# Float64 weights to float32: the high word scaled on ScalarE in place of squared, and one VectorE operation less a piece

## The chip, the cores and the metric

The kernel runs on one core of a Trainium2 chip. A core has TensorE (PE, with its weight loads PEld), VectorE (DVE), ScalarE (ACT), GpSimd (POOL) and SyncE (SP, which here issues all the DMAs), each with an in-order queue of its own; they meet through semaphores. The metric is the time of one execution on the device in microseconds (us). Lower is better.

## The reference

Three stages follow one another. A causal attention (4 batches, 8 heads, 576 positions, head size 64) with a cumulative bias; a mixing block and a feed-forward network (FFN); and a second block of four gated attention experts.

```
x  = attention(q, k, v, s)                       # 4 x 576 x 512
u  = x + ((x^T @ U) @ V)^T                       # mix, rank 32
x  = u + relu(u @ w_ch1) @ w_ch2                 # FFN, 512 -> 2048 -> 512
y  = sum over 2 of 4 experts of gate * (causal attention of x with wq, wk, wv) @ wo
```

`U`, `V`, `w_ch1` and `w_ch2` arrive as float64 (the scale factor of the drawn inputs makes them so) and are used as float32 values. The kernel gets their bits as 64-bit integers.

## The kernel before

**Float64 to float32.** A double has 11 bits of exponent, a float 8. The kernel reads each number as two 32-bit words. The words of a piece of 128 x 256 numbers (the tile `c_raw`, 256 KB) are brought by one DMA. `f32_stages` gives the piece's steps: `s0` (line 103) issues the load; `p0` (line 106, ACT) squares the high word read as a float, into `c_mk`; `p1` (line 109, DVE) keeps the high word where that square is at least a threshold and puts zero elsewhere, into `c_h`; then `v0` to `v4` (lines 113, 118, 122, 127, 131, all DVE) shift the bits up by three, put the two top bits back, isolate sign and exponent into `c_z`, scale the low word by it, and add the two parts. `v5` (ACT, line 198) rounds the sum to the matmul's format (`wh`), and `v6` (POOL, line 201) takes the rest (`wl`): every product is made of three matmuls, wh by x, wl by x and wh by the rest of x.

**The order of the steps.** The pieces form a stream (`f32_stream`). For each piece there are eight steps, by one of two tables: `STREAM` while the first attention runs, `PLAIN` in the FFN. A pair (d, x) in a table is step x of the piece d places ahead: x from 0 is v0 to v6, and -3, -2, -1 are s0, p0, p1. So a load is issued two pieces ahead, and p0 and p1 run one piece ahead.

**Attention stage.** `Attn.run` has 170 iterations (32 heads of 5 row tiles, and 10 more for the lag): scores on PE, masked row minimum on DVE (line 373), exponential on ACT (line 380), normalisation on POOL (line 391), and ten iterations later transposes on PE (lines 403, 406), their eviction, and every tenth iteration the product with V (line 432). Behind each iteration `fillers` puts other work: steps of the stream (one an iteration, two in iterations 41 to 69), preparation of the next head pair, and through `background` tasks of the mix and of the FFN for three of the 16 slices of hidden units (f = 0, 1, 2). An FFN task is a first product of one slice and one chunk of 288 tokens (`hps`, 12 matmuls, line 294) or a second product of one output block (`facc`, 9 matmuls, line 308). A task is only taken when its slice's weights have been wholly converted in program order (`full[f]`); what is left over when iteration 161 comes is put there in one go, ahead of the last transposes.

**FFN stage.** Slices 3 to 15 go in groups of 2, 3, 3, 3 and 2. A slot is one first product (line 826, 12 matmuls) and one second product of an earlier slot (line 844, 12 matmuls); the chunk's four accumulators are evicted by DVE (line 851) after its last slot of the group, and the next chunk's second products wait for that. While one group runs, the next one's weights are converted, and the stream's steps are spread over the slots in proportion (`conv`). The first group of two has 22 slots, 6 of which are left over from slices 0 to 2, and it converts three slices.

A `manual_schedule` keeps the order that the code writes on each engine.

Of the kernel before, what the change touches and what calls it, by code (L numbers as in the profile page):

```python
# [34 lines left out]
HALF = S // 2  # L35
# [10 lines left out]
FA = 3  # L46
GROUPS = [2, 3, 3, 3, 2]

PLAIN = (((0, 0),), ((0, 1),), ((0, 2), (1, -2)), ((0, 3),), ((0, 4), (2, -3)), ((1, -1),), ((0, 5),), ((0, 6),))
STREAM = (((0, 0),), ((-1, 5),), ((0, 1),), ((0, 2), (1, -2)), ((-1, 6),), ((0, 3),), ((0, 4), (2, -3)), ((1, -1),))  # L50
FAST = (40, 70)

ENGA = ('vaaaaa', 'aavaav')
# [14 lines left out]
HIENG = "av"  # L68
BG = (1, 1, 0, 2, 1)
ULF = "vggg"  # L70
TINY = 1.5 * 2.0 ** -15


def cp(nc, eng, out, in_):
# [11 lines left out]
def f32_stages(nc, pool, width, load, m, n, name, use=None, dest=None, fixed={}):  # L86

    t_ = {}  # L90

    def tile_(tag, dt, bufs=1):
        if tag in fixed:
            t_[tag] = fixed[tag][:m, :n].bitcast(dt)
            return t_[tag]
        t_[tag] = pool.tile([P, width], dt, tag=tag, name=f"{tag}_{name}", bufs=bufs)[:m, :n]
        return t_[tag]

    def s0():
        raw = pool.tile([P, width], I64, tag="c_raw", name=f"c_raw_{name}", bufs=2)[:m, :n]  # L100
        load(raw)
        words = raw.bitcast(U32).rearrange("p (n w) -> p n w", w=2)
        t_["low"], t_["high"] = words[:, :, 0], words[:, :, 1].bitcast(F32)

    def p0():
        nc.scalar.activation(out=tile_("c_mk", F32), in_=t_["high"], func=AF.Square)

    def p1():
        nc.vector.scalar_tensor_tensor(out=tile_("c_h", F32), in0=t_["c_mk"], scalar=TINY * TINY,
                                       in1=t_["high"], op0=OP.is_ge, op1=OP.mult)  # L110

    def v0():
        nc.vector.tensor_scalar(out=tile_("c_a", U32, 2), in0=t_["c_h"].bitcast(U32), scalar1=3, scalar2=0x3FFFFFF8,
                                op0=OP.logical_shift_left, op1=OP.bitwise_and)

    def v1():

        nc.vector.scalar_tensor_tensor(out=t_["c_a"], in0=t_["c_h"].bitcast(U32), scalar=0xC0000000, in1=t_["c_a"],
                                       op0=OP.bitwise_and, op1=OP.bitwise_or)

    def v2():
        nc.vector.tensor_scalar(out=tile_("c_z", U32), in0=t_["c_a"], scalar1=0xFF800000, scalar2=None,
                                op0=OP.bitwise_and)

    def v3():

        nc.vector.scalar_tensor_tensor(out=t_["c_h"], in0=t_["low"], scalar=2.0 ** -52, in1=t_["c_z"].bitcast(F32),
                                       op0=OP.mult, op1=OP.mult)

    def v4():  # L130
        nc.vector.tensor_tensor(out=t_["c_a"].bitcast(F32) if use else dest(), in0=t_["c_h"],
                                in1=t_["c_a"].bitcast(F32), op=OP.add)

    def v5():
        if use:
            t_["u"] = use(t_["c_a"].bitcast(F32))
            next(t_["u"])

    def v6():
        if use:  # L140
            next(t_["u"], None)

    return [s0, p0, p1, (v0, v1, v2, v3, v4, v5, v6)]


def f32_stream(jobs, order):

    n = len(jobs)
    for i in range(-2, n + 1):
        for pieces in order:  # L150
            l = [jobs[i + d][3][x] if x >= 0 else jobs[i + d][x + 3] for d, x in pieces if 0 <= i + d < n]
            if l:
                def step(l=l):
                    for f in l:
# [5 lines left out]
def fused_kernel(ctx, tc, qk, v, s, u, vv, w12, wp, out):  # L160
# [349 lines left out]
    with ExitStack() as cx:  # L510
# [699 lines left out]
```

## Time and profile before

| | us |
|---|---|
| time, median of 3 runs | 871.74 |
| lowest and highest run | 869.67, 872.11 |
| profiled execution, first to last instruction (its span) | 870.1 |
| PE, DVE, ACT, POOL busy in it | 814.2, 603.4, 466.9, 310.6 |

The page states no time of its own for the profiled execution beside its span. The span is within the three runs and 1.6 us under their median; the rest of an execution lies around it. A busy PE is not a PE at its peak, since the matmuls overlap in the records: in a stretch without any wait it runs 153 matmuls in 20 us, and the count beside the busy time says more than the share.

### The profile page before, as it was taken

To read this page: it belongs to the slowest core of one execution; us is meant where nothing else is said; L and a number is where in the kernel's file an instruction comes from. 1 tells how busy PE (TensorE), PEld (TensorE's weight loads), DVE (VectorE), ACT (ScalarE), POOL (GpSimd) and SP (SyncE) were. 2 spreads that over 40 slices of the span, in tenths; PEclk is the share of its full clock that TensorE was granted. 3 is DMA by queue.
4 is the path that set the end of the run, shared out by engine and by line. 5 is a ranking of instruction groups with operands and counts; after the bars stand their busy time and mean duration, and the time that the engine had idled before them with its cause. 6 is when DMAs were issued, how large, how long until landed. Compare 5 with 4: busy or idle time off the path is not lost.

```text
span 870.1 us, 17626 instructions
## 1 busy us (share of the span) xinstructions
PE 814.2 (94%) x6068; PEld 747.8 (86%) x6068; DVE 603.4 (69%) x1759; ACT 466.9 (54%) x1384; POOL 310.6 (36%) x468
## 2 busy tenths in 40 slices
PE   3887898999999999999999999999999999999997
PEld 2665676898987889999999999999999988999875
DVE  8687788877687349985885887577446785656541
ACT  6587668866677344323442443333323567666672
POOL 5444255444334324323432342233233123232241
PEclk9898899999999999999999999999999999999999
DMA  7888479687570151111111121112000122112221
GB/s 206 224 212 213 127 187 241 165 210 194 157 195 16 56 188 37 49 50 25 53 48 48 49 61 50 49 43 57 1 1 1 30 42 43 37 55 50 67 64 61
DMA packets 36945, 79.66 MB, mean 92 GB/s; under 512 B 4792, under 2 KB 7992, under 8 KB 36856
## 3 DMA queue, kind: packets, MB, share of 16 engines
q1 hardware_dynamic: 36856, 78.53, 33.7%
q8 instruction: 48, 0.79, 0.4%
q14 instruction: 41, 0.34, 0.1%
HBM read 38.80 MB, written 8.40 MB: 54 GB/s over the span
## 4 chain that ended last, share of the span: by engine, by line
PE 72%; DVE 13%; ACT 5%; DMA 4%; issue 3%; POOL 1%; SPq 1%; DVEq 0%; POOLq 0%; ACTq 0%
PE hps L826 18%; PE facc L844 17%; PE pv L432 9%; PE qkp L1054 5%; PE t L403 4%; PE ops L1077 3%; PE facc L308 3%; PE vps L987 3%; PE qk L362 3%; PE qk L363 2%; PE hps L294 2%; DVE P L373 2%; PE t L406 2%; DMA c_raw_w<-in_w_dram 2%; DMA L<-Cd 2%
## 5 line engine op out<-in xcount | busy, mean ns | idle before, releaser
L278 POOL TENSOR_TENSOR ul<-uT,uh 128x288 fp32r<-128x288 f32 x126 | 103.8, 843 | 175.5 <-ACT uh L277 158.9
L380 ACT ACTIVATE P<-P,stat 64x64 f32<-64x64 f32 (+4 forms) x240 | 133.8, 558 | 43.4 <-DVE stat L373 39.8
L391 POOL TENSOR_SCALAR P<-P,stat 64x64 f32<-64x64 f32 (+4 forms) x160 | 100.9, 646 | 132.0 <-DVE stat L386 88.0
L373 DVE CUSTOM_DVE_ANT_0 P<-qk,mask 64x64 f32<-64x64 f32 (+4 forms) x240 | 116.4, 486 | 45.6 <-PE qk L363 28.8
L362 PE MATMUL qk<-R,L 128*128 128x288 f32 (+4 forms) x288 | 96.7, 340 | 23.1 <-DVE L L573 9.8
L830 ACT ACTIVATE hh<-hps 128x288 fp32r<-128x288 f32 x110 | 44.9, 408 | 135.2 <-PE hps L826 135.0
L76 ACT ACTIVATE pt<-t 64x64 f32<-64x64 f32 (+5 forms) x304 | 89.9, 336 | 42.0 <-PE t L406 36.6
L844 PE MATMUL facc<-hh,wh 128*128 128x288 f32 x376 | 111.2, 296 | 0.6 <-DVE aT L851 0.6
L826 PE MATMUL hps<-uh,wl 128*128 128x288 f32 x376 | 111.2, 296 | 0.0
L826 PE MATMUL hps<-ul,wh 128*128 128x288 f32 x376 | 111.1, 296 | 0.0
L826 PE MATMUL hps<-uh,wh 128*128 128x288 f32 x376 | 111.0, 295 | 0.0
L831 DVE SCALAR_TENSOR_TENSOR hl<-hps,hh 128x288 fp32r<-128x288 f32 x110 | 50.1, 455 | 87.7 <-ACT hh L830 87.4
L844 PE MATMUL facc<-hh,wl 128*128 128x288 f32 x376 | 110.9, 295 | 0.0
L844 PE MATMUL facc<-hl,wh 128*128 128x288 f32 x376 | 110.8, 295 | 0.0
L403 PE MATMUL t<-ident,P 128*128 128x128 f32 x480 | 89.6, 286 | 15.6 <-ACT pt L76 5.6
L363 PE MATMUL qk<-R,L 68*128 68x288 f32 (+9 forms) x288 | 89.1, 315 | 1.2 <-DMA L<-Cd 1.2
L391 POOL TENSOR_SCALAR P<-P,stat,pt 64x64 f32<-64x64 f32 (+4 forms) x80 | 48.5, 620 | 113.3 <-DVE stat L386 57.6
L362 PEld LDWEIGHTS qk<-R,L 128*128 128x128 f32 x288 | 57.3, 199 | 31.3 <-issue 14.9
L403 PEld LDWEIGHTS t<-ident,P 128*128 128x128 f32 x480 | 58.7, 143 | 28.9 <-issue 15.6
L432 PE MATMUL pv<-pt,V 128*64 128x288 f32 (+4 forms) x752 | 80.6, 364 | 0.0
L201 POOL TENSOR_TENSOR wl<-c_a_w,wh 128x256 fp32r<-128x256 f32 x56 | 43.6, 778 | 93.4 <-ACT wh L198 90.9
L432 PEld LDWEIGHTS pv<-pt,V 128*64 128x64 f32 x752 | 52.2, 147 | 27.8 <-issue 7.7
(194 smaller groups left out, 2196.7 us busy)
## 6 DMA issues: line engine op xcount, KB each, us to landing
c_raw_w<-in_w_dram SPq DMA_DIRECT2D x64, 256.0 KB
uT<-in_qk_dram SPq DMA_DIRECT2D x15, 576.0 KB
L<-HI SPq DMA_DIRECT2D x28, 288.0 KB
R<-HI SPq DMA_DIRECT2D x28, 288.0 KB
V<-in_v_dram SPq DMA_DIRECT2D x16, 320.0 KB
R<-uT SPq DMA_DIRECT2D x14, 288.0 KB
L<-uT SPq DMA_DIRECT2D x14, 288.0 KB
aD<-stage SPq DMA_DIRECT2D x6, 576.0 KB
```

The lines of the kernel that those rows point to most:

```text
L76: nc.scalar.activation(out=out, in_=in_, func=AF.Copy)
L278: eng.tensor_tensor(out=l_, in0=src, in1=h_.bitcast(F32), op=OP.subtract)
L362: nc.tensor.matmul(ps[:, bk, :w], lhsT=q1[:, rows], rhs=k1[:, c0:c0 + w], start=True, stop=False)
L363: nc.tensor.matmul(ps[:, bk, :w], lhsT=q2[:, rows], rhs=k2[:, c0:c0 + w], start=False, stop=True)
L373: nc.vector.tensor_tensor_reduce(out=po, in0=view, in1=mk, scale=-1.0, scalar=3.0e38, op0=OP.add, op1=OP.min, accum_out=stat[P - M:, 0, t: ...
L380: nc.scalar.activation(out=po, in_=po, func=AF.Exp, scale=-1.0, bias=stat[P - M:, 0, t:t + 1], accum_out=stat[P - M:, 1, t:t + 1])
L391: nc.gpsimd.tensor_scalar(out=pv, in0=pv, scalar1=stat[r0:, 2, t:t + 1], scalar2=1.0 if gate is None else gate(t)[r0:], op0=OP.mult, op1=O ...
L403: nc.tensor.transpose(ps[:, P * kb:P * kb + P], Pn[:, c0:c0 + P], ident)
L432: nc.tensor.matmul(ps[64 * hh:64 * hh + 64, half, lo - a:e - a], lhsT=V(hh, kb), rhs=pt[:, PST * kb + lo:PST * kb + e], start=kb == 0, sto ...
L826: nc.tensor.matmul(ps, lhsT=w[:, 0, cs], rhs=x, start=i == 0, stop=i == 11)
L831: nc.vector.scalar_tensor_tensor(out=hl, in0=ps, scalar=0.0, in1=hh.bitcast(F32), op0=OP.max, op1=OP.subtract)
L844: nc.tensor.matmul(accs[c][d], lhsT=w[:, 1, cs], rhs=x, start=f == fs[0] and i == 0, stop=f == fs[-1] and i == 2)
```

## The change

`p0` now multiplies the high word, read as a float, by 2^-112 (ACT, `Copy` with a scale), into `c_g`. That takes 112 from the float's exponent field, so that after the shift by three the exponent is a float32's. `p1` is gone, and with it `c_mk`. `v0` only shifts, without the mask that was its second operation, and `v1` puts back one top bit and not two; both read `c_g`. `c_h` is now written by `v3` alone. The tables have seven steps a piece.

```diff
-PLAIN = (((0, 0),), ((0, 1),), ((0, 2), (1, -2)), ((0, 3),), ((0, 4), (2, -3)), ((1, -1),), ((0, 5),), ((0, 6),))
+PLAIN = (((0, 0),), ((0, 1),), ((0, 2), (1, -1)), ((0, 3),), ((0, 4), (2, -2)), ((0, 5),), ((0, 6),))
...
     def p0():
-        nc.scalar.activation(out=tile_("c_mk", F32), in_=t_["high"], func=AF.Square)
-
-    def p1():
-        nc.vector.scalar_tensor_tensor(out=tile_("c_h", F32), in0=t_["c_mk"], scalar=TINY * TINY,
-                                       in1=t_["high"], op0=OP.is_ge, op1=OP.mult)
+
+        nc.scalar.activation(out=tile_("c_g", F32), in_=t_["high"], func=AF.Copy, scale=2.0 ** -112)
 
     def v0():
-        nc.vector.tensor_scalar(out=tile_("c_a", U32, 2), in0=t_["c_h"].bitcast(U32), scalar1=3, scalar2=0x3FFFFFF8,
-                                op0=OP.logical_shift_left, op1=OP.bitwise_and)
+        nc.vector.tensor_scalar(out=tile_("c_a", U32, 2), in0=t_["c_g"].bitcast(U32), scalar1=3, scalar2=None,
+                                op0=OP.logical_shift_left)
...
-    return [s0, p0, p1, (v0, v1, v2, v3, v4, v5, v6)]
+    return [s0, p0, (v0, v1, v2, v3, v4, v5, v6)]
```

`STREAM` loses its `p1` in the same way. Lines behind the change are four lower than before (831 is 827, 851 is 847, 294 is 290).

What moves on DVE, in the FFN's first group, around the eviction of chunk 4 (`facc_4`). The names `c_a`, `c_h`, `c_z`, `c_mk`, `c_raw` are those of the steps above, with the piece's column behind them. Before:

```order
L127 SCALAR_TENSOR_TENSOR c_h_w_0_4579<-c_raw_w_0_4472,c_z_w_0_4635 128x256
L131 TENSOR_TENSOR c_a_w_0_4583<-c_h_w_0_4579,c_a_w_0_4583 128x256
L109 SCALAR_TENSOR_TENSOR c_h_w_256_4643<-c_mk_w_256_4637,c_raw_w_256_4577 128x256
L831 SCALAR_TENSOR_TENSOR hl_4_4659<-hps_4_4645,hh_4_4658 128x288
L851 TENSOR_TENSOR aT<-facc_4_0_4602,aT 128x288
L851 TENSOR_TENSOR aT<-facc_4_1_4603,aT 128x288
L851 TENSOR_TENSOR aT<-facc_4_2_4604,aT 128x288
L851 TENSOR_TENSOR aT<-facc_4_3_4605,aT 128x288
L113 TENSOR_SCALAR c_a_w_256_4682<-c_h_w_256_4643 128x256
L118 SCALAR_TENSOR_TENSOR c_a_w_256_4682<-c_h_w_256_4643,c_a_w_256_4682 128x256
L122 TENSOR_SCALAR c_z_w_256_4685<-c_a_w_256_4682 128x256
L831 SCALAR_TENSOR_TENSOR hl_0_4703<-hps_0_4689,hh_0_4702 128x288
```

The same place now:

```order
L123 SCALAR_TENSOR_TENSOR c_h_w_0_4610<-c_raw_w_0_4446,c_z_w_0_4606 128x256
L127 TENSOR_TENSOR c_a_w_0_4554<-c_h_w_0_4610,c_a_w_0_4554 128x256
L827 SCALAR_TENSOR_TENSOR hl_4_4632<-hps_4_4618,hh_4_4631 128x288
L847 TENSOR_TENSOR aT<-facc_4_0_4574,aT 128x288
L847 TENSOR_TENSOR aT<-facc_4_1_4575,aT 128x288
L847 TENSOR_TENSOR aT<-facc_4_2_4576,aT 128x288
L847 TENSOR_TENSOR aT<-facc_4_3_4577,aT 128x288
L109 TENSOR_SCALAR c_a_w_256_4652<-c_g_w_256_4608 128x256
L114 SCALAR_TENSOR_TENSOR c_a_w_256_4652<-c_g_w_256_4608,c_a_w_256_4652 128x256
L118 TENSOR_SCALAR c_z_w_256_4655<-c_a_w_256_4652 128x256
L123 SCALAR_TENSOR_TENSOR c_h_w_256_4659<-c_raw_w_256_4550,c_z_w_256_4655 128x256
L827 SCALAR_TENSOR_TENSOR hl_0_4675<-hps_0_4661,hh_0_4674 128x288
```

The step between the sum of one piece and the eviction (line 109 of before, with `c_mk`) is gone; nothing else changes places there.

What moves on PE, in iteration 83 of the first attention. `qk` are scores, `t` transposes. Before, iteration 83 ends and iteration 84 begins with no FFN task between them:

```order
L362 MATMUL qk_3_1748<-R_0_121,L_0_119 128x448
L363 MATMUL qk_3_1748<-R_0_124,L_0_122 128x448
L403 MATMUL t_3_1751<-ident,P_114 128x128 x4
L362 MATMUL qk_4_1760<-R_0_121,L_0_119 128x288
L363 MATMUL qk_4_1760<-R_0_124,L_0_122 128x288
```

Now the first product of slice 2 stands there, and behind it the second products:

```order
L358 MATMUL qk_3_1756<-R_0_121,L_0_119 128x448
L359 MATMUL qk_3_1756<-R_0_124,L_0_122 128x448
L399 MATMUL t_3_1759<-ident,P_114 128x128 x4
L290 MATMUL hps_2_1768<-uh_0_1404,wh_1347 128x288
L290 MATMUL hps_2_1768<-ul_0_1405,wh_1347 128x288
L290 MATMUL hps_2_1768<-uh_0_1404,wl_1348 128x288
```

Slice 2's first product moves from iteration 99 to 83. The FFN tasks of the second batch end in iteration 126 and not 129; iterations 127 to 132 have no task of mix or FFN now, and 133 to 150 those of the third batch's mix alone. The third batch's FFN starts in iteration 151 and not 156. Ahead of the last transposes 2 first and 4 second products are left over, where there were 3 and 8. The stream's last conversion step stands near iteration 136, where it stood near iteration 159.

## Rows read from the trace of the kernel before

**Rows 1.** Stages: stretch and length, busy PE, PEld, DVE, ACT, POOL (count), clock, DMA, GB/s.
```profile
10.00:142.00 132.00, 108.86 (x720) 84.88 (x721) 106.97 (x360) 96.81 (x309) 59.14 (x90) 0.91 0.76 198
142.00:165.00 23.00, 20.21 (x156) 16.50 (x153) 18.91 (x64) 19.16 (x64) 12.87 (x21) 1.00 0.93 234
165.00:221.00 56.00, 54.39 (x444) 49.73 (x444) 44.13 (x143) 39.56 (x126) 23.49 (x36) 1.00 0.71 192
221.00:265.00 44.00, 43.29 (x348) 38.46 (x348) 34.45 (x115) 30.56 (x97) 16.54 (x27) 1.00 0.56 150
265.00:300.00 35.00, 33.56 (x260) 29.54 (x257) 19.50 (x57) 16.98 (x52) 13.21 (x21) 1.00 0.09 27
324.00:384.00 60.00, 57.28 (x423) 56.10 (x422) 54.15 (x123) 21.91 (x60) 20.65 (x25) 1.00 0.16 41
384.00:660.00 276.00, 276.00 (x2080) 276.00 (x2079) 191.13 (x453) 101.83 (x275) 91.79 (x116) 1.00 0.15 40
```

**Rows 2.** Who waited for whom on PE, 330 to 400: total us, times, longest.
```profile
PE facc L844 <- DVE aT L851: 1.8, 2, 1.2
PE hps L826 <- DVE hl L831: 0.9, 2, 0.7
```

**Rows 3.** DVE's timeline near 357: start, us, operation, tiles, shape.
```profile
356.77 0.43 DVE L109 SCALAR_TENSOR_TENSOR c_h_w<-c_mk_w,c_raw_w 128x256 f32<-128x256 f32 x1
...
357.48 1.17 DVE L851 TENSOR_TENSOR aT<-facc,aT 128x288 f32<-128x288 f32 x3
```

**Rows 4.** PE's timeline, its two longest waits of that stage [idle before <- releaser].
```profile
345.34 0.40 PE L826 MATMUL hps<-uh,L 128*128 128x288 f32 x1 [0.68 <-DVE hl L831]
...
357.98 0.40 PE L844 MATMUL facc<-hh,L 128*128 128x288 f32 x1 [1.17 <-DVE aT L851]
```

**Rows 5.** The step that goes, by line: busy us, mean ns | idle before.
```profile
L109 DVE SCALAR_TENSOR_TENSOR c_h_w<-c_mk_w,c_raw_w 128x256 f32<-128x256 f32 x44 | 22.6, 514 | 2.3 <-ACT c_mk_w L106 0.5
L109 DVE SCALAR_TENSOR_TENSOR pt<-pt,c_raw_w 128x256 f32<-128x256 f32 x20 | 8.2, 411 | 0.1
```

**Rows 6.** The same line by itself: ns of one, least/median/longest.
```profile
L109 DVE SCALAR_TENSOR_TENSOR c_h_w<-c_mk_w,c_raw_w x44: 407/426/1066, 325.9 to 609.7; 128x256 f32<-128x256 f32 x44
```

**Rows 7.** That line's busy time on DVE from 324 to 384.
```profile
324.00:384.00 60.00, 5.14 (x11) 1.00 0.16 41
```

**Rows 8.** The timeline near 371, POOL beside DVE.
```profile
370.14 2.69 POOL L278 TENSOR_TENSOR ul<-uT,uh 128x288 fp32r<-128x288 f32 x3 [2.82 <-PE hps L826]
...
372.21 0.91 DVE L109 SCALAR_TENSOR_TENSOR c_h_w<-c_mk_w,c_raw_w 128x256 f32<-128x256 f32 x1
```

**Rows 9.** ACT's square and its copy, DVE's two shapes of shift and mask, by line.
```profile
L106 ACT ACTIVATE c_mk_w<-c_raw_w 128x256 f32<-128x256 f32 x44 | 19.1, 435 | 31.9 <-DMA c_raw_w<-in_w_dram 23.7 <-DVE aT L851 3.1 <-DVE c_a_w L113 2.6
L198 ACT ACTIVATE wh<-c_a_w 128x256 fp32r<-128x256 f32 x56 | 23.2, 414 | 54.3 <-DVE c_a_w L131 54.2
L113 DVE TENSOR_SCALAR c_a_w<-c_h_w 128x256 uint32<-128x256 uint32 x44 | 22.9, 521 | 1.6
L122 DVE TENSOR_SCALAR c_z_w<-c_a_w 128x256 uint32<-128x256 uint32 x44 | 14.5, 329 | 1.3
```

**Rows 10.** The chain of waits from 376 to 381: start, us, what.
```profile
376.45 2.98 DMA c_raw_w<-in_w_dram
...
379.54 0.43 ACT c_mk_w L106
379.97 0.31 ACT hh L830
...
380.30 0.46 DVE hl L831
```

**Rows 11.** DVE's row minima (two records an iteration) from 142 to 165: busy us, count.
```profile
142.00:165.00 23.00, 7.83 (x32) 1.00 0.93 234
```

**Rows 12.** One second and one first product of the FFN, from the chain near 225.
```profile
224.79 1.19 PE facc L308 x9
...
226.51 1.62 PE hps L294 x12
```

More of the change, by code (lines that the diff above doesn't have):

```diff
@@ L47 @@
 GROUPS = [2, 3, 3, 3, 2]
-PLAIN = (((0, 0),), ((0, 1),), ((0, 2), (1, -2)), ((0, 3),), ((0, 4), (2, -3)), ((1, -1),), ((0, 5),), ((0, 6),))
-STREAM = (((0, 0),), ((-1, 5),), ((0, 1),), ((0, 2), (1, -2)), ((-1, 6),), ((0, 3),), ((0, 4), (2, -3)), ((1, -1),))
+PLAIN = (((0, 0),), ((0, 1),), ((0, 2), (1, -1)), ((0, 3),), ((0, 4), (2, -2)), ((0, 5),), ((0, 6),))
+STREAM = (((0, 0),), ((-1, 5),), ((0, 1),), ((0, 2), (1, -1)), ((-1, 6),), ((0, 3),), ((0, 4), (2, -2)))
 FAST = (40, 70)
@@ L70 @@
 ULF = "vggg"
-TINY = 1.5 * 2.0 ** -15
 def cp(nc, eng, out, in_):
@@ L105, in p0 @@
     def p0():
-        nc.scalar.activation(out=tile_("c_mk", F32), in_=t_["high"], func=AF.Square)
-    def p1():
-        nc.vector.scalar_tensor_tensor(out=tile_("c_h", F32), in0=t_["c_mk"], scalar=TINY * TINY,
-                                       in1=t_["high"], op0=OP.is_ge, op1=OP.mult)
+        nc.scalar.activation(out=tile_("c_g", F32), in_=t_["high"], func=AF.Copy, scale=2.0 ** -112)
     def v0():
-        nc.vector.tensor_scalar(out=tile_("c_a", U32, 2), in0=t_["c_h"].bitcast(U32), scalar1=3, scalar2=0x3FFFFFF8,
-                                op0=OP.logical_shift_left, op1=OP.bitwise_and)
+        nc.vector.tensor_scalar(out=tile_("c_a", U32, 2), in0=t_["c_g"].bitcast(U32), scalar1=3, scalar2=None,
+                                op0=OP.logical_shift_left)
     def v1():
-        nc.vector.scalar_tensor_tensor(out=t_["c_a"], in0=t_["c_h"].bitcast(U32), scalar=0xC0000000, in1=t_["c_a"],
+        nc.vector.scalar_tensor_tensor(out=t_["c_a"], in0=t_["c_g"].bitcast(U32), scalar=0x80000000, in1=t_["c_a"],
                                        op0=OP.bitwise_and, op1=OP.bitwise_or)
@@ L125, in v3 @@
     def v3():
-        nc.vector.scalar_tensor_tensor(out=t_["c_h"], in0=t_["low"], scalar=2.0 ** -52, in1=t_["c_z"].bitcast(F32),
+        nc.vector.scalar_tensor_tensor(out=tile_("c_h", F32), in0=t_["low"], scalar=2.0 ** -52, in1=t_["c_z"].bitcast(F32),
                                        op0=OP.mult, op1=OP.mult)
@@ L150, in f32_stream @@
         for pieces in order:
-            l = [jobs[i + d][3][x] if x >= 0 else jobs[i + d][x + 3] for d, x in pieces if 0 <= i + d < n]
+            l = [jobs[i + d][2][x] if x >= 0 else jobs[i + d][x + 2] for d, x in pieces if 0 <= i + d < n]
             if l:
@@ L651, in fused_kernel @@
         gap = PST * (NT - 2) + S
-        fixed = {tag: attn.pt[i][:, gap:gap + HALF] for i, tag in enumerate(("c_mk", "c_h", "c_z"))}
+        fixed = {tag: attn.pt[i][:, gap:gap + HALF] for i, tag in enumerate(("c_g", "c_h", "c_z"))}
         def use_u(t):
```

## The prediction

> **What bounds the kernel now.** I read the stages first [rows 1]. The count of matmuls beside the length tells more than the busy share. From 384 to 660 us PE starts 2080 matmuls in 276 us, 7.54 a us, and never waits: there DVE has 191 of 276 us to do, and no shorter DVE step can be seen in the time. From 324 to 384, the FFN's first group, it is 423 in 60 us, where 7.54 a us would be 452. So 29 matmuls, 3.9 us, are lost there, and DVE is busy 54.15 of the 60. Then the waits on PE in that stage [rows 2]: 2.7 us in four waits, all of them for DVE (the count says more than the waits, because overlapping records hide the start of a gap). The two longest stand at 345.3 (0.68 us) and 358.0 (1.17 us) [rows 4]. What DVE did ahead of the second one is in its timeline [rows 3]: at 356.77 it still runs a `p1`, and the first accumulator's eviction starts only at 357.48, though PE has been waiting for it since 356.8. DVE has fallen behind, and the conversion of the next group is what it has done meanwhile.
>
> In the attention stage the picture is mixed [rows 1]: from 10 to 142 PE has 23 us without work, its mean granted clock is 0.91, and DVE (107 of 132), ACT (97) and the DMAs (0.76) are all loaded; from 142 to 165 PE has 2.8 us idle with the DMAs at 0.93; from 165 to 300 only 3.8 us of 135 are left (1.6, 0.7 and 1.4).
>
> **The change part by part.**
>
> *The step that goes.* `p1` is one DVE operation a piece, 67 in all: mean 0.51 us for the 44 in the FFN, 0.41 for the 20 in the attention stage [rows 5], some 32 us with the three of U and V. Of these only what stands where DVE is last counts. From 324 to 384 that is 11 operations and 5.14 us [rows 7]. Six of them, the first at 325.9 [rows 6] and the sixth at 356.77 [rows 3], lie ahead of the wait at 358.0: 6 x 0.43 = 2.6 us of DVE against 0.68 + 1.17 = 1.85 us of PE's two long waits up to there. So DVE is in time at both. DVE's load falls to 49.0 of 60, 82%.
>
> *One wait that DVE doesn't make.* The chain from 376 to 381 [rows 10] is another: a load of 2.98 us issued when v3 has freed the buffer, then ACT's `p0` that waits for it, then `hh` queued behind `p0`, then `hl` on DVE. It takes 0.6 of the 2.7 us, and `p1` has no part in it. I leave it standing. So (2.7 - 0.6)/2.7 of the 3.9 us come back: **-3.0 us**. Bounds: nothing, and all 3.9.
>
> *The square becomes a scaled copy.* Square takes 0.435 us, a plain copy of the same shape 0.414 [rows 9]. Scaled it lies at one or the other: 67 x 0.02 = 1.4 us of ACT at most, and ACT has 22 of 60 us to do in the first group. Taken at nothing; covered by ACT's idle time.
>
> *v0 and v1.* v0 loses its second operation. Its mean is 0.521, that of v2, a shift-and-mask of the same shape with one operation, 0.329 [rows 9]. If the second operation is the cause, that is 0.19 x 11 = 2.1 us of DVE more in the first group, where it would have no more to win than the 0.9 us left of 3.9; if the place in the queue is, nothing. Could it cost? v0 reads what ACT wrote, not DVE; but ACT wrote it five steps earlier. Taken at nothing, -0.9 to 0.
>
> *A wait that is added.* `p0` of the next piece now overwrites `c_g`, which v1 of this piece still reads, and v1 is the step just ahead; before, `c_mk` had been free since `p1`. Behind `p0` on ACT are queued `hh` and `wh`, and for `hh` waits `hl`, for that PE. In the FFN it is hidden as long as the raw words come later than v1: ACT's idle time ahead of its 44 squares is 31.9 us, 23.7 of it put down to that load [rows 9]. Without that cover it is at most one operation of 0.43 us a piece, 11 x 0.43 = 4.7 us on ACT, a wait for PE only when DVE is late. Taken at nothing; if it decides, it takes back the 3.0.
>
> *The load comes nearer.* From `s0` to the same piece's `p0` there are five steps and not six. A slot is 24/7.54 = 3.2 us; the 99 steps of the first group (12 x 8 and 3 to start) over 19 slots are 5.2 a slot, now 87 make 4.6. So 6/5.2 x 3.2 = 3.7 us become 5/4.6 x 3.2 = 3.5, against 2.98 for the load [rows 10]. Half a microsecond is left: nothing, at worst the 3.0 again.
>
> *The attention stage: same pace, earlier end.* The loop still takes one or two steps an iteration. Up to iteration 82 it takes 108 of them; DVE has 5/7 and not 6/8 operations a step, so 3.9 x 0.41 = 1.6 us less, and ACT 2/7 and not 2/8, so 3.9 x 0.435 = 1.7 us more. I call that even; bounds -1.6 and +1.7. What moves is PE's work. Slice 2 is converted sooner, so its tasks start in iteration 83 and not 99, into the stretch from 142 to 165 where PE has 2.8 us to spare, and 1 first and 4 second products fewer stand ahead of the last transposes: 1.62 + 4 x 1.19 = 6.4 us [rows 12]. But work that is moved is not work that is gone; only idle time that it fills is won. And the stretch behind it is thinned out: 24 iterations (127 to 150) have no FFN task, and 6 of them nothing at all. Such bare iterations run at 23/16 = 1.44 us [rows 11] with 12% of PE idle [rows 1]: 24 x 1.44 x 0.12 = 4.2 us, where the same iterations have about 0.7 now (221 to 265). With the mix in 18 of the 24, I take half of it, +2.1 - 0.7 = +1.4. Of the 2.8 us that are filled I take half too, -1.4, because DVE and ACT (19 of 23 each) and the DMAs are near their own ends there. **0**, from -2.8 to +3.5.
>
> *Sum.* The span 870.1 - 3.0 + 0 = 867.1. It stands 1.6 us under the median of the runs, which I put on top: **868.7 us**, 0.35% under 871.74. What a measurement of this kernel can tell from no change is 0.3%, 2.6 us.
>
> **A rule that speaks against it.** The step at 372.21 took 0.91 us beside POOL's subtractions [rows 8], with a median of 0.43 [rows 6]. The Trainium skill (SBUF — State Buffer, Who interferes with whom) says that a VectorE instruction with two SBUF inputs and a GpSimd one that reads SBUF take turns, and the second to come is blocked until the first is done; the trace agrees by that row. By that rule the 0.48 us over the median were a turn of POOL's that the next two-input step inherits, so 5.14 us would be 4.7, and a block moved to just ahead of an eviction would leave up to 0.5 us of a wait: 869.2.
>
> **The rivals.**
> - *The attention stage gains too.* The FFN tasks fill all 2.8 us, and the thinned stretch stays as full as 221 to 265 is now. For it: PE's idle time of 142 to 165 is in the very iterations. Against: the DMAs at 0.93. 867.1 - 2.8 + 1.6 = 865.9.
> - *The wait in the FFN only changes its name.* ACT's `p0` waits for v1 or for the nearer load, `hh` behind it, and PE loses the same 3 us to `hl`. For it: the chain of rows 10 is there already, and half a microsecond is thin. Against: PE never waits after 384 though ACT waits there as well. 871.7.
> - *Slower: the thinned stretch costs more than the first group gives back.* Place: iterations 127 to 150. None of the 2.8 is filled, 4.2 - 0.7 = 3.5 us of idle come in, and the granted clock falls between its two levels (2.4 and 1.2 GHz) as it does from 10 to 142, where the mean is 0.91 and PE had idled before: 24 x 1.44 = 35 us at 0.91 give 3.2 us. 867.1 + 3.5 + 3.2 + 1.6 = 875.4. It decides as soon as the clock goes down there and nothing was filled; against it, the clock stays at 1.00 from 142 on, at the same idle share.
>
> **How the numbers follow.** The forecast 0.42 (its own range 867.0 to 869.8: the wait of rows 10 gone as well, or the rule's block), the attention stage gains 0.20, the wait changes its name 0.28, slower 0.10. The range that leaves out no more than 2 in 10 goes from 864.7 (the second case with something of v0 or of the steps before 142) to 872.8 (the third with a little of the fourth). Faster by over 0.3% is under 869.1: four fifths of the forecast and all of the second case, 0.34 + 0.20 = 0.54. Slower is the last, 0.10. Within 0.3%: 0.36.
>
> **What would show it.** In the profile of the changed kernel: PE's waits for DVE in the FFN's first group fall from 2.7 us to under 1, and its count there comes near 452 in 60 us; DVE falls from 90% to about 82% busy; the stretch from the first product of the group to the end of the group is 3 us shorter. The attention stage should end within 2 us of the present time: earlier by 3 speaks for the first rival. `hh` waiting behind `p0` with PE waiting for `hl` speaks for the second, a clock under 1.00 between iterations 127 and 150 for the third. The forecast is wrong if PE keeps its waits in the first group with DVE under 85% busy, or if the attention stage moves by more than the first group does.

## The result: slower, 882.84 us

The changed kernel took 882.84 us (median of 4 runs, 881.11 to 885.18), the kernel before beside it 871.92 (869.67 to 873.42): 1.0137 times as long, 95% interval 1.0116 to 1.0158. The forecast was 868.7, the range ended at 872.8. Changes in us below are ratios times 871.74.

**Where the 11.7 us of the spans (881.8 - 870.1) arise.** The FFN stage begins with the first product that writes `hps` on line 826 (now 822). In PE's timeline of the kernel before, and then of the changed one:

```profile
309.64 0.40 PE L826 MATMUL hps<-uh,L 128*128 128x288 f32 x1 [0.77 <-ACT uT L76]
```

```profile
322.88 0.40 PE L822 MATMUL hps<-uh,L 128*128 128x288 f32 x1 [0.78 <-ACT uT L75]
```

The attention stage has become 13.2 us longer. From there to the end of the last first product it is 358.8 us before and 356.8 after: the FFN gives back 2.0; the rest takes 0.4 more. So the FFN gained, two thirds of what was forecast, and the attention stage, which was forecast to stay, took all of that and much more. And it took it early. The first row minimum of iteration 80 stands on DVE at 138.22 before and at 151.87 after, though the first FFN task changes places in iteration 83:

```profile
138.22 0.23 DVE L373 CUSTOM_DVE_ANT_0 P<-qk,mask 64x64 f32<-64x64 f32 x1
```

```profile
151.87 0.23 DVE L369 CUSTOM_DVE_ANT_0 P<-qk,mask 64x64 f32<-64x64 f32 x1
```

From there to 309.64 it was 171.4 us, and now, to 322.88, 171.0. These spans are of one execution each; E4 below shows how far two of them can differ (1.8 us).

The stages of the changed kernel, columns as in [rows 1], the bounds moved by 13:

```profile
10.00:155.00 145.00, 115.04 (x723) 90.73 (x724) 106.27 (x357) 98.30 (x313) 59.77 (x92) 0.86 0.72 183
155.00:178.00 23.00, 22.92 (x185) 21.38 (x185) 14.76 (x49) 14.17 (x44) 11.77 (x18) 1.00 0.68 180
...
337.00:397.00 60.00, 58.91 (x439) 58.15 (x438) 49.37 (x118) 21.68 (x61) 20.22 (x25) 1.00 0.17 45
397.00:673.00 276.00, 276.00 (x2079) 276.00 (x2079) 172.02 (x416) 102.69 (x277) 91.94 (x118) 1.00 0.14 39
```

The same 720 matmuls of the first stage now take 145 us and not 132, and no engine is fuller for it: DVE 106 us, ACT 98, DMAs 0.72 where they were 0.76. The granted clock is 0.86 and not 0.91. All engines wait more. What for, ACT's waits for loads from 10 to 300 tell (total us, times, longest), before and after:

```profile
ACT HI L489 <- DMA uT<-in_qk_dram: 9.5, 7, 2.0
ACT pt L106 <- DMA c_raw_w<-in_w_dram: 3.1, 5, 1.5
ACT pt L106 <- DMA c_raw_v<-in_vv_dram: 2.6, 1, 2.6
```

```profile
ACT pt L106 <- DMA c_raw_w<-in_w_dram: 11.5, 5, 4.4
ACT HI L485 <- DMA uT<-in_qk_dram: 4.2, 4, 1.7
ACT pt L106 <- DMA c_raw_v<-in_vv_dram: 1.2, 1, 1.2
```

Line 106 is `p0` (in the attention stage `c_g` lies in `pt`). It comes up before its raw words are there. (In part the new waits stand in for others: ACT's waits for `uT`, the operands of the next head pair, fell from 9.5 to 4.2 us.) The longest of the waits of `p0`, in the timelines of SP, ACT, DVE, POOL and PE of the changed kernel (start, us, operation, idle before and its releaser):

```profile
52.98 0.48 SPq L458 DMA_DIRECT2D L<-HI  x1
53.52 2.14 SPq L458 DMA_DIRECT2D R<-HI  x2
55.70 0.83 SPq L458 DMA_DIRECT2D L<-HI  x1
56.98 1.08 SPq L183 DMA_DIRECT2D c_raw_w<-in_w_dram  x1
58.19 1.10 SPq L458 DMA_DIRECT2D R<-uT  x1
...
58.92 0.22 ACT L75 ACTIVATE pt<-t 64x64 f32<-64x64 f32 x1
63.59 0.43 ACT L106 ACTIVATE pt<-c_raw_w 128x256 f32<-128x256 f32 x1 [4.45 <-DMA c_raw_w<-in_w_dram]
63.93 0.76 ACT L376 ACTIVATE P<-P,stat 128x576 f32<-128x576 f32 x1
...
64.69 0.41 ACT L75 ACTIVATE pt<-t 128x128 f32<-128x128 f32 x2
...
64.81 0.17 DVE L381 TENSOR_SCALAR stat<-stat 128x5 f32<-128x5 f32 x1 [4.66 <-ACT P L376]
...
65.40 2.84 POOL L387 TENSOR_SCALAR P<-P,stat 64x64 f32<-64x64 f32 x5 [6.91 <-DVE stat L382]
...
65.20 0.87 PE L399 MATMUL t<-ident,P 128*128 128x128 f32 x3 [5.09 <-issue]
```

The load is issued at 56.98, behind four transfers of 288 KB, and its words are there by 63.59: 6.6 us, where a load in the FFN took 2.98 [rows 10]. The Trainium skill (DMA: Bandwidth & Descriptors, Two DMAs through the same engine are not ordered) says that the pieces of transfers on one queue of a DMA engine start in the order of issue; this row is in keeping with that, and so are the waits that E9 and E16 below leave with loads of half the size; no run tests the order itself. ACT stands 4.45 us. Behind `p0` on ACT stand the exponential of the attention (L376) and the eviction of the last transposes (L75). For the exponential wait DVE's reciprocal and, behind that, POOL's normalisation. PE's next transposes start at 65.20, 0.1 us after that eviction has ended and before the normalisation starts at 65.40. The profile names no releaser of PE's wait (`issue`); by these times it was the eviction. PE is idle for 5.09 us, and the clock falls from 1.00 towards its lower level of 1.2 GHz (two overlapping windows, columns as above):

```profile
52.00:64.00 12.00, 7.34 (x62) 5.61 (x61) 6.50 (x23) 6.45 (x21) 4.42 (x6) 1.00 0.83 179
62.00:72.00 10.00, 6.80 (x39) 5.88 (x41) 5.83 (x23) 7.56 (x25) 2.75 (x5) 0.66 0.58 152
```

In the kernel before the same piece's load goes out at 62.10, `p0` runs at 66.64 and waits for nothing (ACT has just waited 1.94 us for `uT`), and the clock of 62 to 72 is 0.83.

Three numbers of a piece matter here, all read from the table `STREAM`: its **steps** (8 before, 7 now: the pace), the steps from `s0` to the same piece's `p0` (the **distance**: 5 before, 4 now), and the steps an iteration: one, but two in 41 to 69, where 5 steps are 2.5 iterations and 4 are 2.

The wait of 4.45 us stands ahead of that fast stretch. By the table the piece's load belongs to iteration 30 and its copy to 34; SP issues the load only at 56.98, when DVE has begun iteration 33. The four other waits for W, 7.1 us in all, lie in iterations 41 to 69. So the first row minima of iterations 35, 40, 70 and 80 stand 0.3 us earlier than before, then 4.4, 8.7 and 13.65 later. The last 4.9 us come where `p0` waits for nothing; there the clock is low, where before it was 1.00 from 130 to 140. That this follows from the waits ahead of it is likely and not shown:

```profile
132.00:140.00 8.00, 7.23 (x44) 4.67 (x42) 4.78 (x18) 2.73 (x9) 4.09 (x6) 0.57 0.49 110
```

### The profile page after: what moved, and what is told of

Same layout as the page of the kernel before. It is cut to its first block, busy times and chain, and to the rows that moved or that the text cites. A ratio compares the mean times of both kernels' runs of the same rounds, so it can differ in the third digit from the quotient of the medians.

```text
span 881.8 us, 17496 instructions
## 1 busy us (share of the span) xinstructions
PE 820.4 (93%) x6068; PEld 756.3 (86%) x6068; DVE 571.0 (65%) x1692; ACT 466.9 (53%) x1384; POOL 307.6 (35%) x468
## 4 chain that ended last, share of the span: by engine, by line
PE 72%; DVE 10%; DMA 5%; issue 4%; ACT 4%; POOL 3%; SPq 1%; POOLq 0%; DVEq 0%; ACTq 0%
PE facc L840 19%; PE hps L822 18%; PE pv L428 7%; PE qkp L1050 5%; PE t L399 4%; PE hps L290 3%; PE ops L1073 3%; PE qk L359 3%; PE qk L358 3%; PE vps L983 2%; PE facc L304 2%; DMA L<-uT 2%; PE t L402 2%; DVE P L369 2%; POOL P L387 2%
## 5 line engine op out<-in xcount | busy, mean ns | idle before, releaser
L376 ACT ACTIVATE P<-P,stat 64x64 f32<-64x64 f32 (+4 forms) x240 | 133.7, 557 | 42.6 <-DVE stat L369 40.2
L358 PE MATMUL qk<-R,L 128*128 128x288 f32 (+4 forms) x288 | 99.2, 349 | 22.2 <-DVE L L569 9.8
L75 ACT ACTIVATE pt<-t 64x64 f32<-64x64 f32 (+5 forms) x304 | 89.9, 335 | 45.7 <-PE t L402 38.2
L399 PE MATMUL t<-ident,P 128*128 128x128 f32 x480 | 91.5, 291 | 21.1 <-issue 9.8
L359 PE MATMUL qk<-R,L 68*128 68x288 f32 (+9 forms) x288 | 91.4, 322 | 0.5 <-DMA L<-Cd 0.4
L399 PEld LDWEIGHTS t<-ident,P 128*128 128x128 f32 x480 | 60.7, 146 | 33.7 <-issue 21.3
L358 PEld LDWEIGHTS qk<-R,L 128*128 128x128 f32 x288 | 59.3, 206 | 30.1 <-issue 15.8
L428 PE MATMUL pv<-pt,V 128*64 128x288 f32 (+4 forms) x752 | 83.0, 372 | 0.8 <-DVE stat L369 0.8
```

What stands on the lines that cost most here:

```text
L75: nc.scalar.activation(out=out, in_=in_, func=AF.Copy)
L358: nc.tensor.matmul(ps[:, bk, :w], lhsT=q1[:, rows], rhs=k1[:, c0:c0 + w], start=True, stop=False)
L359: nc.tensor.matmul(ps[:, bk, :w], lhsT=q2[:, rows], rhs=k2[:, c0:c0 + w], start=False, stop=True)
L376: nc.scalar.activation(out=po, in_=po, func=AF.Exp, scale=-1.0, bias=stat[P - M:, 0, t:t + 1], accum_out=stat[P - M:, 1, t:t + 1])
L399: nc.tensor.transpose(ps[:, P * kb:P * kb + P], Pn[:, c0:c0 + P], ident)
L428: nc.tensor.matmul(ps[64 * hh:64 * hh + 64, half, lo - a:e - a], lhsT=V(hh, kb), rhs=pt[:, PST * kb + lo:PST * kb + e], start=kb == 0, sto ...
```

## The experiments

Theory A: `p0` is reached too soon behind its load. Rivals: B or P, the pace (more loads and steps in the same time, another order on SP); C, the copy itself or its wait for `v1`; M, the FFN tasks that moved. Beside each run stood runs of the kernel before, and the times are read by the ratio to them. A ratio is known to 1.1 to 1.8 us on either side, a difference of two ratios to about 2 (an estimate from the intervals given). The diffs show the line that matters; `(1, 7)` is a step that does nothing.

**E1, an empty eighth step.** It restores pace and distance without `p1`.

```diff
-... ((0, 3),), ((0, 4), (2, -2)))
+... ((0, 3),), ((0, 4), (2, -2)), ((1, 7),))
```

> The changed kernel with an empty eighth step in the table of the attention stage: the kernel before's pace of loads and its five steps (two and a half fast iterations) from the raw load to the scaled copy are back, p1 stays away. The FFN's table has seven steps as changed. Theory A (ACT comes to the scaled copy before its raw load has landed, everything behind it on ACT waits, PE idles and the clock falls): 868 to 870 us, the attention stage ends at 310 us again, ACT's waits of L106 for c_raw from 10 to 300 fall from 11.5 to about 3 us. Theory B (seven steps load the same bytes in fewer iterations, the denser loads delay the tiles R and L): the same 868 to 870, so this run does not part A and B. Theory C (the scaled copy itself or its new wait for v1 costs the time): 880 to 883, as the changed kernel.

867.93 us, ratio 0.9968 (0.9952 to 0.9983), first FFN product at 307.2; ACT's wait for W's words is 3.3 us. C falls: copy, `v1` and the lost `p1` are all in this kernel, and so is the added wait, 4.4 us of `p0` for DVE in the attention stage. What makes the change slow is the rhythm: pace, distance and what moves with them.

**E2, the copy two steps later, seven steps.** Distance 6.

```diff
-... ((0, 2), (1, -1)), ((-1, 6),), ((0, 3),), ...
+... ((0, 2),), ((-1, 6),), ((0, 3), (1, -1)), ...
```

> The changed kernel with its seven steps and its pace, but the scaled copy two steps later in the attention stage's table: six steps from the load to the copy and not four. Order and density of the loads on SP stay as changed. Theory A (the copy is reached before its load): about 870 us, or lower if the earlier end of the conversion is worth something; ACT's waits of L106 for c_raw in 10 to 300 at 3 us or less; first FFN product near 310. Theory B (denser loads, or the other order on SP, delay R and L): 880 to 883, first FFN product near 322. Theory C (the copy or its wait for v1): 880 or more, since the copy now stands directly behind v1's step.

872.08 us, 1.0009 (0.9993 to 1.0025); first FFN product at 309.7. Moving one step of ACT takes back 11 of the 11.9 us. But 4 are missing to E1, ACT still waits, and PE waits 8.3 us for the tile `L` (2.7 before). The two lines are of an execution of 870.3 us:

```profile
ACT pt L106 <- DMA c_raw_w<-in_w_dram: 6.4, 4, 2.3
...
PE qk L358 <- DMA L<-uT: 8.3, 4, 3.6
```

**E3, the kernel before with its square one step earlier.** Distance 4, eight steps, `p1` kept.

```diff
-... ((0, 1),), ((0, 2), (1, -2)), ...
+... ((0, 1), (1, -2)), ((0, 2),), ...
```

> The kernel before, with p1 and eight steps, but its squaring one step earlier in the attention stage's table: four steps from the load to the square and not five, at the unchanged pace of loads. Nothing of the change is in it. Theory A: slower, 876 to 882 us, with ACT's waits of L106 for c_raw in 10 to 300 near 10 us and the first FFN product 5 to 12 us later than 310. Theories B and C: 871 to 873, unchanged.

875.85 us, 1.0048 (1.0031 to 1.0066); 4.2 us slower, a little under what theory A gave. A loss of this kind can be had without anything of the change, by the distance alone. The trace is of the longest of the six executions (880.42 us), so its waits may be longer than usual:

```profile
ACT pt L106 <- DMA c_raw_w<-in_w_dram: 8.7, 5, 3.9
ACT pt L106 <- DMA c_raw_v<-in_vv_dram: 4.0, 1, 4.0
```

**E4, the change in the FFN alone.** The attention stage converts as before (square, `p1`, eight steps).

```diff
+    if old:
+        return [s0, q0, q1, (w0, w1, v2, w3, v4, v5, v6)]
     return [s0, p0, (v0, v1, v2, v3, v4, v5, v6)]
```

> The change in the FFN stage alone: the attention stage converts as before (square, p1, eight steps), the conversions of the FFN's groups use the scaled copy and seven steps. If the two stages are independent and the first group gains what the traces show (2.0 us): 869.9 us, first FFN product at 310, the first group 2 us shorter than before. If the gain of the first group is an artefact of the later, disturbed start: 871.9. If the FFN part itself loses: above 873.

868.95 us, 0.9971 (0.9958 to 0.9984), 2.5 us faster. The FFN's gain is real and of its own. The first FFN product stands at 307.8, 1.8 us earlier than before with the same instructions ahead of it: so far do two executions of that stage differ, and smaller differences of single traces there tell nothing.

**E7, E1 with the copy two steps later.** Eight steps, distance 7.

```diff
-... ((0, 2), (1, -1)), ((-1, 6),), ((0, 3),), ((0, 4), (2, -2)))
+... ((0, 2),), ((-1, 6),), ((0, 3), (1, -1)), ((0, 4), (2, -2)), ((1, 7),))
```

> The changed kernel with the empty eighth step and, besides, the scaled copy two steps later: seven steps from load to copy at the pace of before. Theory A alone (only the distance from load to copy counts): the last 4.7 us that ACT waits for the raw words of pieces 5 to 13 fall to 2 or less, and the time goes below the 867.9 of the kernel with the empty step alone, to 864 to 867. If five steps were enough at this pace: 867 to 869, the same as without the later copy, and what parts the seven-step kernel with the late copy (872.1) from it is the pace. If the copy, now nearer ahead of v0, holds up DVE: above 869.

**863.94 us**, 0.9909 (0.9896 to 0.9923): faster than both kernels, and than the one before by 7.9 us. ACT's waits for W are nearly gone, and the first stage's clock is 0.95 where it was 0.91 (E4, with the stream of before, has 0.94, so the clock of one trace proves little):

```profile
ACT pt L106 <- DMA c_raw_v<-in_vv_dram: 1.9, 1, 1.9
ACT pt L106 <- DMA c_raw_w<-in_w_dram: 0.4, 1, 0.4
...
10.00:142.00 132.00, 109.53 (x760) 86.82 (x760) 111.27 (x370) 103.62 (x334) 66.13 (x99) 0.95 0.82 212
```

**E8, E2 with the moved FFN tasks held** until iteration 98.

```diff
-            ffn = ffnq and full.get(ffnq[0][0]) == 2 * DM
+            ffn = ffnq and full.get(ffnq[0][0]) == 2 * DM and not 80 < turn[1] < 98
```

> The seven-step kernel with the late copy (872.1 us), but the FFN tasks that its earlier conversion lets start in iterations 83 to 97 are held until iteration 98, where the kernel before starts them. Theory M (the 4 us that it stands over the kernel with the empty step are the price of the moved work): 868 to 869. Theory P (they are the price of the denser loads in iterations 41 to 69, before any task moves): 871 to 873, iteration 80 at 140 us as without the hold. If the move was a gain that hid a larger loss: above 873.5.

876.08 us, 1.0045 (1.0032 to 1.0058). Holding them costs 3.1 us against E2: there the move was a gain, and M falls. From iteration 80 to the first FFN product E2 needs 169.1 us, E8 172.9.

**E9, the changed kernel with half of each raw load** of W in the attention stage.

```diff
-                nc.sync.dma_start(out=raw, in_=w12[f, :, x, c:c + width])
+                w = width // 2 if fixed else width
+                nc.sync.dma_start(out=raw[:, :w], in_=w12[f, :, x, c:c + w])
```

> The changed kernel, seven steps and four steps from load to copy, but in the attention stage each raw load of W brings half of its columns, which are used twice; half of the weights of those slices is left out that way, the instructions on ACT and DVE keep their sizes. Theory A (the copy comes ahead of its load's landing): a load of half the bytes lands sooner, the waits of ACT for raw words in pieces 5 to 13 fall from 11.7 to under 5 us, and most of the 11.4 us come back: 868 to 874. If what delays the load is not its bytes and those beside it but the turn of the issue on SP: ACT's waits stay, 878 to 883. Theory C (cost of the copy or of its wait for v1): 881 to 884.

877.4 us, 1.0060 (1.0047 to 1.0072): between the cases. Half of the bytes give back 6.7 of 11.9 us, so the size of these loads has a large part in the loss; but ACT still waits 7.4 us for W's words, so size isn't all of it. The rest fits the load's place in the queue, which this run doesn't test.

**E10, E2's stream two iterations later.**

```diff
-                if i >= 4 and convs:
+                if i >= 6 and convs:
```

> The seven-step kernel with the late copy, its stream of steps started two iterations later (at 6, not 4), so that every raw load stands at another place among the loads of the operand tiles. Theory P as a matter of density: 871 to 873, PE's waits for L and R in 10 to 310 as without the shift (10.5 us). If it is a matter of which load happens to stand ahead of which operand tile on SP: another time by more than 2 us, either way (868 to 870 or 874 to 877), with PE's waits for L and R changed by as much.

873.07 us, 1.0014 (0.9996 to 1.0031), PE's wait for `L` 6.7 us. No better and no worse: other pieces wait, as long in all (6.0 us for W).

**E11, the kernel before with its square two steps later.** Distance 7, `p1` kept.

```diff
-... ((0, 2), (1, -2)), ((-1, 6),), ((0, 3),), ...
+... ((0, 2),), ((-1, 6),), ((0, 3), (1, -2)), ...
```

> The kernel before, with p1 and all its operations, its squaring two steps later in the attention stage's table: seven steps from load to square, p1 two steps behind it. Nothing of the change is in it. If the 7.6 us that the changed kernel with the empty step and the late copy gained are mostly the place of ACT's step: 871.6 less 4 to 6, so 865.5 to 868 (the 2.1 us of the FFN and some of p1 in the attention stage stay out). If they need the change, because p1 now follows the square more closely and waits: 870 to 873.

867.98 us, 0.9952 (0.9934 to 0.9971). The control for E7: 4.2 of its 7.9 us could be had without the change. The other 3.7 are the change's: 2.5 in the FFN (E4), and 1.2 in the attention stage, which is within the noise.

**E12, seven steps with distance 7**, the copy in the step of the next piece's load.

```diff
-... ((0, 2), (1, -1)), ((-1, 6),), ((0, 3),), ((0, 4), (2, -2)))
+... ((0, 2),), ((-1, 6),), ((0, 3),), ((0, 4), (1, -1), (2, -2)))
```

> The changed kernel with its seven steps, the scaled copy three steps later, beside the issue of the load after next: seven steps from load to copy, as in the kernel with the empty step and the late copy (863.9), v0 directly behind it. If the distance is all: 864 to 867. If the pace of seven steps has a price of its own even where the copy waits for nothing: 869 to 873. If v0 right behind the copy makes DVE wait for ACT: above 873.

872.65 us, 1.0006 (0.9992 to 1.0020). No better than distance 6, and ACT waits 7.0 us. In seven steps more distance doesn't help further. It isn't a clean test: right behind the copy, `v0` waits for it 3.3 us in three waits. That the pace has a price of its own is seen better from E2: it has one step of distance more than E1 and is 3.6 us slower.

**E13, E1 with the copy one step earlier.** Eight steps, distance 4, no `p1`.

```diff
-... ((0, 1),), ((0, 2), (1, -1)), ...
+... ((0, 1), (1, -1)), ((0, 2),), ...
```

> The changed kernel with the empty eighth step, the scaled copy one step earlier: four steps from load to copy, as in the changed kernel, at the pace of before. With the kernel before's own early square (875.8, four steps with p1) it shows the price of distance at this pace without p1. Theory A with a price that the pace doesn't change: 867.9 + 11 = 879. If four steps cost at this pace what they cost the kernel before (4.3 us over its five): 871 to 874, and the rest of the changed kernel's loss is the pace. If p1 was what made four steps bad: 868.

876.93 us, 1.0057 (1.0041 to 1.0073): 7.8 us over E1, between the two cases. Here `p0` stands right behind `v1`, so the added wait is in it as well (5.8 us of ACT's idle time ahead of `p0` are put down to DVE, 11.7 to the words of W and V).

**E14 and E15, the copy alone in the eighth step.** Distance 9. In E14 the first piece's copy had come ahead of the second load, and ACT stood 4.4 us for U's words at the start; E15 mends that.

```diff
-... ((0, 2), (1, -1)), ((-1, 6),), ((0, 3),), ((0, 4), (2, -2)))
+... ((0, 2),), ((-1, 6),), ((0, 3),), ((0, 4), (2, -2)), ((1, -1),))
```

> The changed kernel with eight steps in the attention stage, the scaled copy alone in the eighth, the place that p1 had: nine steps from load to copy, v0 right behind it. If more distance still helps: under 863.5. If seven steps are enough and v0 has time behind the copy: 863 to 865, as with seven. If v0 waits for ACT there: 866 or more.

> As the run before with the copy in the eighth step (nine steps from load to copy), but the first two loads are issued in the old order: there the copy of the first piece had come up ahead of the second load, and the start of the kernel lost 4 to 6 us with ACT waiting for U's words. If seven steps from load to copy are enough: 863 to 866. If more distance still helps: 859 to 863. If v0 right behind the copy costs DVE its turn: 867 to 870.

871.72 us, 0.9998 (0.9981 to 1.0015), and 870.34, 0.9975 (0.9955 to 0.9995), with runs from 865 to 874. Nine steps are worse than seven, though in E15 ACT waits for no raw words at all. So the wait for the words is not the only thing that the copy's place sets. What else it sets was not settled; the copy stands right ahead of `v0`, which reads it, but DVE waits for it only 0.3 us in either trace.

**E16 and E17, half of each raw load of W** in E2 and in E7.

```diff
-                nc.sync.dma_start(out=raw, in_=w12[f, :, x, c:c + width])
+                w = width // 2 if fixed else width
+                nc.sync.dma_start(out=raw[:, :w], in_=w12[f, :, x, c:c + w])
```

> The seven-step kernel with the late copy (six steps; 872.1 us), with half of each raw load of W in the attention stage left out and the loaded half used twice; half of those weights is missing from the result. Theory P-bytes (the denser loads hold up the operand tiles and each other on the DMA queues): PE's waits for L and R in 10 to 310 fall from 10.5 to 5 us or less, and 4 to 8 us come back: 864 to 868, clearly more than the same halving gives the eight-step kernel. Theory P-steps (more of ACT's and POOL's work per step): 869 to 872.

> The control: eight steps with the empty one, seven steps from load to copy (863.9 us), with the same half of each raw load of W left out. P-bytes: little is left to win, 861 to 864. If the halving helps here as much as in the seven-step kernel, the bytes don't part the two paces: 856 to 860.

870.66 us, 0.9994 (0.9974 to 1.0013), and 862.84, 0.9893 (0.9872 to 0.9913): 1.3 us for E2, 1.4 for E7, both within the noise. The bytes don't part the two paces. Nor do PE's waits for its operands: for `L` they fell from 8.3 us in E2 to 3.5 in E16, and the time hardly followed; and E7, the fastest, has 5.1 for `L` and 3.2 for `R`. In E16 ACT still waits 5.4 us, once 3.3, for loads of half the size.

**E18 to E20, the pace of the fast stretch.** Seven steps outside iterations 41 to 69, the copy with distance 6; inside, E18 takes an empty step after every piece (8 steps, distance 7), E19 after every second (7.5, distance 6 or 7), E20 two (9, distance 7).

```diff
+                    if convs[0].empty and not FAST[0] < i < FAST[1]:
+                        convs.pop(0)
                     convs.pop(0)()
```

> The eight-step kernel with the late copy (863.9 us), its empty step taken only in iterations 41 to 69 and skipped elsewhere: seven steps a piece where the loop takes one step an iteration. If the price of the pace arises in the fast stretch alone, and the earlier end of the conversion, with FFN tasks that start sooner, is worth the 3 to 4 us that holding them cost: 860 to 863. If the pace costs as much where one step an iteration is taken: 865 to 870.

> As the kernel whose empty step is taken in the fast stretch alone (866.7 us), but there only after every second piece: seven and a half steps a piece in iterations 41 to 69, seven elsewhere, six or seven steps from load to copy. If the price follows the pace: half way to the 872 of seven steps, 868.5 to 870.5. If it depends on which iterations the pieces fall in, and four iterations a piece happen to fit the loop of five and the loads of a pair of heads: 872 or more, no better than seven steps.

> The same with two empty steps a piece in the fast stretch: nine steps there, seven elsewhere, still seven from load to copy. If the price follows the pace: 861 to 865.5, faster than with eight. If eight fits by its place and not by its pace: 868 or more.

866.66 us, 0.9939 (0.9921 to 0.9957); 872.13, 1.0013 (0.9999 to 1.0026); 864.3, 0.9913 (0.9896 to 0.9929). E20 equals E7 within the intervals. The price arises mostly in the fast stretch, but not evenly: 7 and 7.5 steps cost the same, 8 take 6.5 us less, 9 some two less again, which the intervals hardly part. That speaks for a part of the iteration in which a piece falls; no run tests that by itself. In E20 V's first load goes out at 20.54 us and not at 10.46, since an empty step took its place among the two steps issued ahead of the loop; the longer of its two waits for V, 2.5 us, comes from that. ACT's waits in E12, E19 and E20:

```profile
ACT pt L106 <- DMA c_raw_w<-in_w_dram: 7.0, 3, 3.4
```

```profile
ACT pt L110 <- DMA c_raw_w<-in_w_dram: 9.4, 6, 2.3
```

```profile
ACT pt L110 <- DMA c_raw_v<-in_vv_dram: 3.9, 2, 2.5
ACT pt L110 <- DMA c_raw_w<-in_w_dram: 1.6, 3, 0.7
```

**The loss put together**, along one chain of runs. The rows are differences within that chain, so their sum has to come out and tests nothing:

| from, to | what differs | us |
|---|---|---|
| before, E1 | the new operations, no `p1` (2.5 of it in the FFN, E4) | -2.8 |
| E1, E13 | distance 5 to 4; the copy now right behind `v1` | +7.8 |
| E13, changed kernel | eight steps to seven; the copy one step farther from `v1` | +7.0 |
| sum | measured: 11.9 | +12.0 |

So the split between distance and pace is rough. In the kernel before, where `p0` doesn't wait for `v1`, one step of distance cost 4.2 us (E3). The third row holds a gain of some 3 us for the moved FFN tasks, if they are worth here what they are in E2 (E8); then the pace itself costs about 10, an estimate. Through which wait the pace costs that stays open: the bytes of the loads don't part the paces (E16, E17). The share of the clock in both was not parted from the waits that come before its falls.

## Why the prediction was wrong

- **The attention stage** is the step that failed: "Up to iteration 82 ... I call that even; bounds -1.6 and +1.7", in the part that ended with "**0**, from -2.8 to +3.5". It counted DVE's and ACT's operations a step. They were even enough; what it left out, and so put at nothing, was the rhythm, +13.65 us by iteration 80: ACT's waits for W's words rose from 3.1 to 11.5 us. DVE's density is no cause: E11 has three DVE operations in four steps and is faster than E2 with five in seven.
- **The load comes nearer** was seen, and priced for the FFN's table alone. There it held: the one wait of PE for `hl` that is left, 0.5 us, comes by a `wh` and not by a load (see below). The same loss of a step, five to four, was never worked out for `STREAM`, where the loads share the queue with the attention's tiles, two steps an iteration make four steps two iterations in 41 to 69, and the exponential stands behind `p0`. That [rows 1] showed the DMAs at 0.76 and the clock at 0.91 there was noted, and not taken as a sign that a late load would cost most in this place. Nor was SP's queue followed: that the load of the long wait now stands right behind the four transfers of `HI`, where `uT` and `Cd` had come between, could have been seen in the order.
- **The moved FFN tasks** were taken at -1.4, with +1.4 for the thinned stretch. In E2's rhythm the move was worth about 3 us (E8), near the 2.8 of the first rival, though by a difference known to 2 us; in the changed kernel it wasn't measured. The rival on the slower side had the right sign and the wrong place: its stretch of iterations 127 to 150 kept a clock of 1.00 (221:265 and 265:300 of the changed kernel). Its 3.2 us for 35 us at 0.91 should be 3.5, which changes nothing.
- **The FFN's first group** gained near to what was forecast, by other waits than forecast. Its -3.0 measured -2.0 in the traces (the stretch to the last first product is 356.7 or 356.8 us in all 17 runs with seven steps in the FFN, 358.8 to 359.1 in the three with eight) and -2.5 in E4 (interval 1.4 to 3.7). DVE fell to 49.37 of 60, the 82% forecast; the count rose to 439 and not 452. PE's waits there, once [rows 2], are now

```profile
PE facc L840 <- DVE aT L847: 0.6, 1, 0.6
PE hps L822 <- DVE hl L827: 0.5, 1, 0.5
```

The sum "6 x 0.43 = 2.6 us of DVE against 0.68 + 1.17" took both long waits of [rows 4] as gone, and the 0.6 of the chain of [rows 10] as what stays. It is the other way round. The two that remain are those of [rows 4], at the 249th and the 333rd matmul from the first product on, shortened from 0.68 and 1.17 to 0.52 and 0.58; and the third, at the 501st, is gone; so it is in all 17 traces. Before, the third; now, the two:

```profile
381.27 0.37 PE L844 MATMUL facc<-hh,wh 128*128 128x288 f32 x1 [0.61 <-DVE aT L851]
```

```profile
357.96 0.40 PE L822 MATMUL hps<-uh,L 128*128 128x288 f32 x1 [0.52 <-DVE hl L827]
...
370.00 0.40 PE L840 MATMUL facc<-hh,L 128*128 128x288 f32 x1 [0.58 <-DVE aT L847]
```

DVE has no backlog there, as forecast: it idles 0.78 us ahead of both `hl`. What is late is ACT's `hh`, though its product on PE had ended near 355.3: it stands behind a `wh`, and that has waited for DVE's `v4` (L127), here and again at 368.38:

```profile
356.70 0.42 ACT L194 ACTIVATE wh<-c_a_w 128x256 fp32r<-128x256 f32 x1 [3.31 <-DVE c_a_w L127]
357.02 0.39 ACT L826 ACTIVATE hh<-hps 128x288 fp32r<-128x288 f32 x1
...
357.45 0.46 DVE L827 SCALAR_TENSOR_TENSOR hl<-hps,hh 128x288 fp32r<-128x288 f32 x1 [0.78 <-ACT hh L826]
```

So the conversion still reaches PE, through `wh` on ACT, a way that the sum didn't have; and that -2.0 came near -3.0 is in part luck. By the Trainium skill's rule that the prediction weighed (SBUF — State Buffer, Who interferes with whom) it was 2.5; no run here tests the rule itself.

- **The added wait** of `p0` for `v1` came and was covered, as priced. ACT's waits from 337 to 397:

```profile
ACT c_g_w L106 <- DVE c_a_w L114: 13.2, 6, 3.4
ACT c_g_w L106 <- DMA c_raw_w<-in_w_dram: 5.7, 3, 2.0
```

13.2 us in six waits. PE's wait for `hl`, the way by which they would reach it, is 0.5 us in all, and that one comes behind a `wh`.

- **Copy and Square** cost the same, and `v0` got shorter in the FFN, in all of the changed kernel (compare [rows 9]):

```profile
L106 ACT ACTIVATE c_g_w<-c_raw_w 128x256 f32<-128x256 f32 x44 | 19.2, 436 | 54.4 <-DVE c_a_w L114 29.4 <-DMA c_raw_w<-in_w_dram 14.1 <-issue 10.3
L109 DVE TENSOR_SCALAR c_a_w<-c_g_w 128x256 uint32<-128x256 uint32 x44 | 18.2, 413 | 0.5 <-ACT c_g_w L106 0.5
```

## What to carry to other kernels

A step taken out of a rotation shortens every distance in it: work out load to first use anew for each table that uses the rotation, in iterations and in time, and look where the load then stands in SP's queue. Where an engine's next work serves a critical chain, a load's first use belongs well behind the load; in E11 two steps later were worth 4.2 us, where the operation saved 2.8 (E1). Later is not always better: right ahead of its consumer (E12, E14, E15) the copy gained nothing more or lost. And to price a change apart from the rhythm that it brings, pad it to the old rhythm (E1), and give the old kernel the merit of a better rhythm too (E11).

## What the runs showed of the hardware

A load of 256 KB took 2.98 us in the FFN and, issued behind four transfers of 288 KB, 6.6 in the attention stage; loads of half the size were waited for as well (5.4 us in all, E16). And the second operation of `v0` cost nothing that can be seen: in the attention stage its 20 instructions took 316 ns with two operations and 321 with one. So the fall from 521 to 413 ns in the FFN isn't the operation either. There the least is 273 ns before and 277 now, the longest 933 and 932; 22 of 44 took 600 ns or more before, 10 of 44 now. What makes them long wasn't looked into. The two groups of the attention stage, before and after:

```profile
L113 DVE TENSOR_SCALAR c_a_w<-pt 128x256 uint32<-128x256 uint32 x20 | 6.3, 316 | 1.2 <-DVE pt L109 0.5
```

```profile
L109 DVE TENSOR_SCALAR c_a_w<-pt 128x256 uint32<-128x256 uint32 x20 | 6.4, 321 | 2.8 <-POOL wl L197 2.8
```
